# The opening of a fused attention and mixer kernel: batch 0's steps in another order, and no stuffing matmuls

## The chip, the cores and the metric

The kernel runs on one core of one Trainium2 chip. The metric is device time in microseconds (us) of one launch. Before the change it is 648.35 us, the median of three runs (647.37 to 651.1). The engines are called PE (matrix engine), ACT (scalar engine), DVE (vector engine), POOL (GpSimd) and SP (the engine that only issues DMA here).

## The reference, cut to what matters

Attention in chunks of 32 tokens is followed by a mixer. There are 4 batches, 8 heads, 768 tokens, a head size of 64 and 8 memory tokens.

```python
for c in range(nc):                      # chunks of 32; 16 tokens of left, 8 of right context
    k_full = concat([mem_k, k[:, :, l_start:r_end]]); v_full = concat([mem_v, v_ctx])
    scores = scale * (q_c @ k_full.T)
    a = exp(scores - max(scores)); a = a / (sum(a) + 1e-9)
    out[:, :, c] = a @ v_full
x = out.transpose(0, 2, 1, 3).reshape(B, S, 512)
h = x.T @ U @ V                          # U: 768 x 32, V: 32 x 768, double precision inputs
u = x + h.T
result = u + relu(u @ w_ch1) @ w_ch2     # 512 -> 2048 -> 512, double precision inputs
```

U, V and the two weight matrices arrive as 64-bit numbers. The kernel decodes them to 32 bits on the chip with integer and multiply operations.

## The kernel before, in words

The kernel has a front, in which the attention of batch 0 is computed, and a long rest, in which the mixer of one batch runs beside the attention of the next. The front is the function `attention` with `b == 0`. It handles batch 0 in three parts T = 0, 1, 2 of 256 tokens, each with two halves h of four heads.

For each part the front goes through these steps. `regroup` lays out the raw k or q. `turn` transposes it on PE into a PSUM bank. `k_part` copies it to the context tile `kall` with ACT (lines 664 to 672), and `q_part` copies q (line 688). In `k_part` the copy at line 668 writes "edges": the first tokens of part T that are the right context of the last block of part T - 1. `s_turn` computes scores of one part on PE (line 708). `s_weights` takes the maximum and subtracts it on DVE (lines 730 and 731) and takes the exponential on ACT (line 734). `s_sums` sums rows on DVE (lines 739 to 744). `t_part` transposes one half of the probabilities on PE (line 762) and copies them with ACT (line 765). `av_part` multiplies with v on PE (line 782) and scales into the tiles x on DVE (line 794); each part gives two tiles x of 128 tokens.

With x the front goes on to the mixer. `collect(t)` (line 806) adds u times one x tile to the accumulator acc2. `turn_x` (line 1151) turns the first three x tiles, 12 matmuls, into the banks ps_h, ps_h, acc0 and acc1, and `turn_x1` (line 1175) the other three for one column block. `spread_v` (lines 292 to 298) copies the decoded v of the mixer onto three partition groups. `join_uT` (lines 1160 to 1165) joins the turned x with g, the collected product (lines 1100 and 1101); `join_uT1` does so for the second half (lines 1192 to 1197). The first hidden products follow (line 1501).

The class `Words` decodes 64-bit numbers: `begin` on ACT (line 240), `shift`, `power` and `mantissa` on DVE (lines 247, 255, 260), `join` (line 267). U, V and the weights pass through it. The weights go through the generator `stream`; `advance(n)` makes n steps of it. Step 1 is `begin` of the first weights, steps 2 to 5 decode them and write the upper part (line 397), the next step writes the lower part (line 401).

The order of the work is written out in the front. PE and SP keep the order of the program everywhere. ACT and POOL keep it in the front and for the first two units of the mixer (`HEAD`), DVE for the first 27 (`PACED`); after that a planner with its own estimates orders them. PSUM banks in the front come from a fixed cycle: `cyc = ["a", "h", "a", "o0", "a", "h", "o1"]`, where a is a pool of three banks ps_a, h a pool of two banks ps_h, and o0 and o1 are acc0 and acc1. Once `wide[0]` is set to None, all banks come from ps_a.

Stuffing matmuls multiply a tile of zeros. `keep_clock(n)` asks for n of them, and the next `att_ps()` puts them in front of its own work (line 143). There are 12 at the very start (`START`), two before the scores of part 0, two before those of part 1, two before the last product with v (`GAP`), and eight before `turn_x1` (`CHAIN[0]`).

The loads are issued by SP in the order of `LOADS`: q and k of the three parts, u and v of the mixer, the attention's v of the parts 0, 1 and 2 (v0, v1, v2, lines 610 and 617), then weights (lines 344 and 356). `take(n)` issues the next n of this list.

## Time and profile before

| | us |
|---|---|
| median of three runs | 648.35 |
| the three runs | 651.1, 647.37, 648.35 |
| the profiled execution's own time | 648.01 |
| its span, first to last instruction | 645.9 |
| PE busy | 619.7 |
| DVE busy | 379.5 |
| ACT busy | 252.5 |
| POOL busy | 137.5 |

All times of the trace count from the start of the span. A wait carries the name of what ended it. "issue" stands for time in which the engine waited for nothing that the profile shows. Ends of matmuls are modelled, so neighbouring matmuls overlap by a few tenths of a microsecond in a timeline.

### The profile page before, as it was taken

Reading aid. Unit: us, or ns where it says so; the run is one execution under the profiler, and the core shown is the slowest. Engines: PE = TensorE matmul, PEld = TensorE weight load, DVE = VectorE, ACT = ScalarE, POOL = GpSimd, SP = SyncE. Lnnn points to the kernel's source line nnn. Section 1 sums busy time; section 2 is a strip of 40 time slices with the busy share of each in tenths; the row PEclk is TensorE's granted clock in tenths of the full one; section 3 lists DMA queues with packets and bytes.
Section 4 is the critical chain, followed back from the end, with each engine's and each line's share of the span. In section 5 each row is a group of like instructions: output and inputs, shape, how many; then the busy total and the mean of one; then the engine's idle time right before and its main releaser. Section 6 shows DMA issues by size and latency. Waiting matters only on the chain.

```text
span 645.9 us, 15115 instructions
## 1 busy us (share of the span) xinstructions
PE 619.7 (96%) x6006; PEld 536.3 (83%) x6006; DVE 379.5 (59%) x727; ACT 252.5 (39%) x635; POOL 137.5 (21%) x292
## 2 busy tenths in 40 slices
PE   7788999999899999899999999999999999999997
PEld 5557999988787888779889798998877899999886
DVE  6948788798783737954755834653456732222322
ACT  5525445448332535522255613321247621221221
POOL 5100000043154454312734100202325200000000
PEclk9899999999999999999999999999999999999999
DMA  8895576667888699576589759767422065565201
GB/s 240 160 335 200 170 253 231 224 184 179 184 187 214 167 298 280 179 188 162 169 244 207 160 158 284 228 175 200 117 68 96 0 185 175 146 175 155 96 0 49
DMA packets 168705, 115.02 MB, mean 178 GB/s; under 512 B 100956, under 2 KB 139484, under 8 KB 168636
## 3 DMA queue, kind: packets, MB, share of 16 engines
q1 hardware_dynamic: 168012, 113.92, 62.3%
q8 instruction: 47, 0.77, 0.5%
q10 hardware_dynamic: 624, 0.15, 0.1%
q14 instruction: 22, 0.18, 0.1%
HBM read 90.83 MB, written 28.97 MB: 185 GB/s over the span
## 4 chain that ended last, share of the span: by engine, by line
PE 74%; DVE 9%; DMA 6%; ACT 5%; issue 2%; POOL 2%; SPq 1%; ACTq 0%; POOLq 0%; DVEq 0%
PE ps_h L1321 23%; PE acc L1552 18%; PE acc L1562 9%; PE ps_h L1501 9%; PE ps_a L782 2%; DMA blocks<-spread 2%; PE ps_a L1552 2%; ACT uc L171 1%; PE acc L1546 1%; PE ps_a L708 1%; DMA w1l<-w1s 1%; PE ps_a L1562 1%; POOL pt L171 1%; DVE x L1517 1%; PE acc L806 1%
## 5 line engine op out<-in xcount | busy, mean ns | idle before, releaser
L1552 PE MATMUL acc<-w,hh 128*128 128x512 f32 x612 | 157.9, 393 | 1.3 <-ACT hh L1335 1.3
L1552 PEld LDWEIGHTS acc<-w,hh 128*128 128x128 f32 x612 | 113.3, 188 | 22.8 <-ACT hh L1335 2.8
L1562 PE MATMUL acc<-w,hl 128*128 128x512 f32 x306 | 86.9, 392 | 0.0
L1562 PEld LDWEIGHTS acc<-w,hl 128*128 128x128 f32 x306 | 56.9, 188 | 11.9
L1321 PE MATMUL ps_h<-t12h,w1l 128*128 128x384 f32 x192 | 55.5, 343 | 0.7 <-ACT c L1347 0.6
L1321 PE MATMUL ps_h<-bh,w1l 128*128 128x384 f32 x192 | 53.0, 340 | 0.0
L171 POOL COPY pt<-y 32x128 f32<-32x128 f32 x96 | 30.1, 314 | 98.5 <-DVE y L168 94.3
L1321 PE MATMUL ps_h<-t34h,w1l 128*128 128x384 f32 x152 | 46.1, 344 | 0.2 <-ACT hst L1347 0.2
L171 POOL COPY uc<-y 32x128 f32<-32x128 f32 x96 | 32.6, 340 | 56.8 <-DVE y L168 53.1
L1501 PE MATMUL ps_h<-uh,w1h 128*128 128x384 f32 x124 | 42.5, 347 | 2.2 <-ACT w1h L397 1.2
L1501 PE MATMUL ps_h<-ul,w1h 128*128 128x384 f32 x124 | 41.4, 338 | 0.4 <-DVE ul L1197 0.4
L1336 DVE SCALAR_TENSOR_TENSOR hl<-ps_h,hh 128x384 fp32r<-128x384 f32 x29 | 16.1, 554 | 43.0 <-ACT hh L1335 42.8
L1343 DVE TENSOR_TENSOR c<-ps_h,c 128x384 f32<-128x384 f32 x19 | 10.5, 554 | 49.7 <-PE ps_h L1321 49.7
L1321 PEld LDWEIGHTS ps_h<-t12h,w1l 128*128 128x128 f32 x192 | 35.3, 188 | 3.7 <-ACT c L1347 1.0
L1336 DVE SCALAR_TENSOR_TENSOR hl<-hst,hh 128x384 fp32r<-128x384 f32 x36 | 20.6, 574 | 30.0 <-PE acc L1562 21.3
L1321 PE MATMUL ps_h<-b,w1l 128*128 128x384 f32 x174 | 35.5, 339 | 0.7 <-DVE hst L1343 0.7
L1321 PEld LDWEIGHTS ps_h<-bh,w1l 128*128 128x128 f32 x192 | 35.1, 188 | 0.8
L1335 ACT ACTIVATE hh<-ps_h 128x384 fp32r<-128x384 f32 x29 | 14.2, 491 | 53.0 <-PE ps_h L1321 52.8
L1343 DVE TENSOR_TENSOR hst<-ps_h,hst 128x384 f32<-128x384 f32 x36 | 19.9, 553 | 23.8 <-ACT hst L1347 16.8
L1335 ACT ACTIVATE hh<-hst 128x384 fp32r<-128x384 f32 x36 | 18.8, 524 | 36.4 <-PE acc L1552 30.0
L1347 ACT COPY c<-ps_h 128x384 f32<-128x384 f32 x19 | 9.1, 479 | 59.5 <-PE ps_h L1321 59.5
L1321 PE MATMUL ps_h<-t12l,w1l 128*128 128x384 f32 x96 | 32.4, 337 | 0.0
(253 smaller groups left out, 1278.9 us busy)
## 6 DMA issues: line engine op xcount, KB each, us to landing
w1l<-w1s SPq DMA_DIRECT2D x155, 256.0 KB
rw<-in_moe_w_ch_dram SPq DMA_DIRECT2D x14, 512.0 KB
out_dram<-x SPq DMA_DIRECT2D x24, 256.0 KB
blocks<-spread SPq DMA_DIRECT2D x24, 256.0 KB
vb<-in_v_dram SPq DMA_DIRECT2D x56, 98.0 KB
raw<-in_moe_w_ch_dram SPq DMA_DIRECT2D x20, 256.0 KB
rw<-in_moe_w_ch_dram SPq DMA_DIRECT2D x16, 256.0 KB
w1s<-sums SPq DMA_DIRECT2D x16, 256.0 KB
```

Of the source, the lines that this page charges most:

```text
L171: (nc.scalar.copy if both and (5 * to + at) % 8 < 3 else nc.gpsimd.tensor_copy)(out=dst[CK * to:CK * to + CK, :, CK * at:CK * at + CK], in ...
L708: nc.tensor.matmul(out=psv[s][(slice(CK * i, CK * i + CK), t) + ((p // 2, p % 2) if b >= DIRECT else (p % 2, p // 2))], lhsT=qt[p // 2][ro ...
L782: nc.tensor.matmul(out=psv[g][CK * i:CK * i + CK, t, j], lhsT=pt[s][rows, 2 * t + k_, CK * i:CK * i + CK], rhs=vt[rows, NI * t + i, D * j: ...
L806: nc.tensor.matmul(out=gp[0][0:96], lhsT=u3[:, t].rearrange("p g r -> p (g r)"), rhs=xs[(b, t)], start=(t == 0), stop=(t + 1 == NT),)
L1321: nc.tensor.matmul(out=ps[:, :TOK], lhsT=w_, rhs=u, start=(start and m == 0), stop=(m == 5), skip_group_check=True,)
L1335: nc.scalar.activation(out=hh, in_=c, func=AF.Relu)
L1336: nc.vector.scalar_tensor_tensor(out=hl, in0=c, scalar=0.0, in1=hh.bitcast(F32), op0=ALU.max, op1=ALU.subtract,)
L1343: nc.vector.tensor_tensor(out=out, in0=ps[:, :TOK], in1=in1, op=ALU.add)
L1347: nc.scalar.copy(out=out, in_=ps[:, :TOK])
L1501: nc.tensor.matmul(out=ph[:, :TOK], lhsT=w[:, c, :], rhs=u[c], start=(m == 0), stop=(m + 1 == len(parts)),)
L1552: nc.tensor.matmul(out=acc[tt], lhsT=h[:, sl], rhs=w, start=(begins and m == 0), stop=False,)
L1562: nc.tensor.matmul(out=acc[tt], lhsT=hl[:, sl], rhs=w2h[f], start=False, stop=ends is not None)
```

## The change

The instructions that compute are the same, apart from 14 stuffing matmuls that are left out: 2, 2, 2 and 8. The 12 at the start stay.

- `k_part` is split. `k_edges` turns a half of k on PE and, for T > 0, copies the edges. `k_main` makes the other copies. For parts 1 and 2 the edges of both halves are now copied before the rest of either half.
- The row sums of part 0 and the beginning of u's decoding move behind the softmax of part 1. The rest of u's decoding moves behind the softmax of part 2, around the product with v of part 0.
- The product with v of part 1 comes directly after the turning of part 1's probabilities. Four `collect` follow it, then the row sums of part 2 and v's decoding, and only then the turning of part 2's probabilities. In the kernel before, v's decoding came ahead of that product's scaling on DVE, and the turning of part 2 ahead of the first collects.
- `turn_x` comes before `spread_v`, and `wide[0] = None` between them, so `spread_v` takes its three banks from ps_a.
- `advance(1)` and `advance(4)` become one `advance(5)` behind `spread_v`, ahead of the last product with v.

```diff
-GAP = [2, 2, 2]
-CHAIN = [8, 4]
...
+            k_main(T, h, k_edges(T, h))
+
+        def k_edges(T, h):
             psv = turn(kn.pop((T, h)))
+            m, w = NM // 2, CK // 2
+            last = kall[:, NB * ((T + 1) % 2) + NB - 1].rearrange("c p (n r) -> c p r n", r=2)
+            p = slice(2 * h, 2 * h + 2)
+            if T > 0:
+                nc.scalar.copy(out=last[:, p, :, m + w:], in_=psv[:, :, :, 0, 0:NW // 2 - m - w])
+            return psv
+
+        def k_main(T, h, psv):
             copy = nc.scalar.copy
...
             for h in two:
                 q_part(0, h)
+            made = [k_edges(1, h) for h in two]
             for h in two:
-                k_part(1, h)
+                k_main(1, h, made[h])
...
-            keep_clock(GAP[0])
             sc = s_turn(0)
             for h in two:
                 q_part(1, h)
+            made = [k_edges(2, h) for h in two]
             for h in two:
                 s_weights(0, *sc, [h])
-                k_part(2, h)
-            u_words.begin()
-            s_sums(0)
+                k_main(2, h, made[h])
             yield
-            keep_clock(GAP[1])
             sc = s_turn(1)
             for h in two:
                 q_part(2, h)
+            s_weights(1, *sc)
+            s_sums(0)
+            u_words.begin()
+            yield
+            sc = s_turn(2)
+            for s in two:
+                t_part(0, s)
+            s_weights(2, *sc)
             u_words.shift()
             u_words.low()
+            av_part(0)
             nc.vector.tensor_copy(
...
             nc.gpsimd.tensor_copy(out=u_sb, in_=u3[:, :, 0, :])
-            s_weights(1, *sc)
-            yield
-            sc = s_turn(2)
-            for s in two:
-                t_part(0, s)
-            s_weights(2, *sc)
-            v_words.begin()
             s_sums(1)
-            av_part(0)
             yield
             for s in two:
                 t_part(1, s)
+            v_words.begin()
+            av_part(1)
+            take(len(loading))
+            for t in range(4):
+                collect(t)
             s_sums(2)
             v_words.shift()
             v_words.low()
             val = v_words.join()
-            av_part(1)
-            take(len(loading))
             for s in two:
                 t_part(2, s)
-            for t in two:
-                collect(t)
+            early = turn_x(range(NCK))
+            wide[0] = None
             spread_v(val)
             yield
-            advance(1)
-            for t in two:
-                collect(2 + t)
-            early = turn_x(range(NCK))
-            wide[0] = None
-            keep_clock(GAP[2])
-            advance(4)
+            advance(5)
             av_part(2)
             yield
             advance(1)
             for t in range(4, NT):
                 collect(t)
-            keep_clock(CHAIN[0])
             turned.extend(turn_x1(c) for c in range(3))
```

## Rows read from the trace of the kernel before

**Rows 1.** The page's head and first part: busy time by engine.

```profile
span 645.9 us, 15115 instructions
PE 619.7 (96%) x6006; PEld 536.3 (83%) x6006; DVE 379.5 (59%) x727; ACT 252.5 (39%) x635; POOL 137.5 (21%) x292
```

**Rows 2.** Busy time by stretch: stretch, length, engines, granted clock, DMA share and GB/s.

```profile
0.00:60.00 60.00, 47.77 (x972) 34.57 (x973) 41.77 (x100) 26.98 (x77) 11.62 (x22) 0.97 0.82 240
...
sum 646.00, PE 619.70 PEld 536.31 DVE 379.55 ACT 252.53 POOL 137.47; mean PE 47.67 PEld 41.25 DVE 29.20 ACT 19.43 POOL 10.57
```

**Rows 3.** Chain of waits, 0 to 62 us: start, duration, what.

```profile
28.94 0.96 issue
...
41.06 0.43 PE ps_a L143 x2
41.49 1.48 PE ps_a L782 x91
42.98 0.75 DVE x L794 x2
...
45.73 1.73 PE ps_a L143 x8
...
49.46 0.19 PE ps_h L1160
```

**Rows 4.** Timeline of PE: start, duration, instruction; idle time before it in brackets.

```profile
18.29 0.24 PE L708 MATMUL ps_a<-kall,qt 64*32 64x64 f32 x1 [1.23 <-ACT kall L668]
...
31.33 0.66 PE L762 MATMUL ps_a<-ident,pt 128*128 128x128 f32 x4
33.57 0.60 PE L762 MATMUL ps_h<-ident,pt 128*128 128x128 f32 x4 [1.59 <-issue]
...
35.82 0.45 PE L292 MATMUL ps_a<-dec,rep 32*96 32x256 f32 x1
...
36.43 0.67 PE L806 MATMUL acc<-x,uarea 128*96 128x512 f32 x1
```

**Rows 5.** Timeline of ACT: copy of part 1's second half of turned probabilities.

```profile
28.49 0.58 ACT L765 COPY pt<-ps_a 128x512 f32<-128x512 f32 x1
```

**Rows 6.** Timeline of DVE.

```profile
18.65 0.26 DVE L247 TENSOR_SCALAR dec<-dec 128x192 int32<-128x192 int32 x1 [0.26 <-ACT dec L240]
...
20.23 0.46 DVE L894 COPY uarea<-dec 128x576 f32<-128x576 f32 x1
...
29.36 1.27 DVE L739 TENSOR_REDUCE rs<-pt 128x8 f32<-128x512 f32 x2
...
32.42 0.41 DVE L794 TENSOR_TENSOR x<-ps_h,rs 128x256 f32<-128x256 f32 x1
...
37.27 0.41 DVE L298 TENSOR_TENSOR v<-acc,v 32x256 fp32r<-32x256 f32 x1
...
39.84 0.69 DVE L267 TENSOR_TENSOR dec<-dec 128x512 f32<-128x512 f32 x1
...
47.02 0.42 DVE L1101 TENSOR_TENSOR g<-acc,g 32x256 fp32r<-32x256 f32 x1 [0.43 <-ACT g L1100]
```

**Rows 7.** Timelines of SP's DMA issues and of POOL.

```profile
6.57 1.94 SPq L552 DMA_DIRECT2D kraw<-in_k_dram  x2
...
19.81 5.11 SPq L610 DMA_DIRECT2D vb<-in_v_dram  x8
...
11.83 1.36 POOL L577 COPY kn<-kraw 128x512 f32<-128x512 f32 x2 [2.52 <-DMA kraw<-in_k_dram]
...
18.89 0.40 POOL L636 COPY kall<-memkT 128x256 f32<-128x256 f32 x1 [0.90 <-PE ps_h L708]
```

**Rows 8.** Busy time and granted clock by stretch, as in rows 2.

```profile
21.20:24.60 3.40, 1.66 (x54) 1.21 (x39) 3.18 (x7) 1.87 (x4) 0.40 (x1) 1.00 0.74 146
24.60:28.00 3.40, 3.40 (x134) 3.17 (x135) 3.25 (x8) 2.00 (x5) 0.00 (x0) 0.50 1.13 173
...
31.40:34.80 3.40, 1.81 (x10) 1.22 (x11) 2.36 (x7) 1.17 (x2) 0.00 (x0) 1.00 0.70 192
```

## The prediction

> **What bounds the kernel now.** I read four views. The page comes first [rows 1]: TensorE (PE) is busy for 619.7 of 645.9 us, so the kernel as a whole is bound by PE and little can be won elsewhere. Then the table by stretches [rows 2], for where PE is not busy: in the first 60 us it works 47.77 us, and in the 586 us behind them 619.70 - 47.77 = 571.9 us. So 12.2 us of idling lie in the front, which the change rewrites, and 14.1 us behind it. Behind 60 us PE runs almost without a gap, so what the front gains or loses in time is kept to the end. Third, the chain of waits through the front [rows 3]; the reader is to see which pieces of it are stuffing (L143), which are waits called "issue", and where it passes to the vector engine (DVE). I take as the front's end mark the first matmul of line 1160, at 49.46 us in that chain: there the turned x of batch 0 meets g, and from there the instructions and their order are the same in both kernels. The forecast is how far this mark moves. Last, each engine's timeline around these pieces [rows 4 to 7] and the granted clock [rows 8].

> I count against the profiled execution's own 648.0 us (a span of 645.9 us and 2.1 us around it). It lies 0.34 us under the median of the three runs, 648.35.

> **Edges of k first, u's decoding later.** Today PE stalls 1.23 us before the last scores of part 1, until ACT has copied the edges of k's third part (L668), which stand behind a softmax and ten other copies [rows 4]. The edges now come first, so this stall goes. The decoding of u takes DVE from 18.65 to 20.69 us, ahead of part 1's softmax [rows 6]; it moves behind the softmax of part 2. Nothing is added: four edge copies and five decode operations are moved. With both out of the way, and the row sums of part 0 behind the second softmax too, I put part 1's turned probabilities some 3 us earlier: today the last of their copies ends at 28.49 + 0.58 = 29.07 us [rows 5], so about 26 us.

> What is late next? The product with v of part 1 also needs that part's v. Its eight transfers are issued until 19.81 + 5.11 = 24.92 us [rows 7], and nothing in the change moves them. No row says when the last one lands. The nearest rows are two transfers of k, issued between 6.57 and 8.51 us, for which POOL waits until 11.83 us [rows 7]: 3.3 to 5.3 us from issue to use. So v is there between 28.2 and 30.2 us. I take 29.65, near the late end, because the first product, today held to 29.90 by an "issue" wait [rows 3], can have had little to spare. So of the 3 us only a little arrives. Today the product restarts at 29.90 and PE is free for the next step at 31.33 [rows 3, 4]: 1.43 us for about 7/8 of it. In the new kernel three of its four head groups of the first half run while the last transfer comes, and 5/8 are left, 0.9 us: free at 30.55. Gain 0.78 us; from 0 to 1.5 us with the bounds of the landing and the stalls of today.

> **Products first, then the third part's turning.** Today PE then turns part 2's first half, waits 1.59 us on "issue" before the second half [rows 4], and does two collects, the spreading of v, two collects and the turning of x, until the stuffing at 41.06 [rows 3]. The new order is four collects, both halves, turning of x, spreading. The bank of the second half was released long before 33.57, so I read the 1.59 us as PE's own instruction stream; the four collects, slow and few, now stand in its place, and I count it as gone (kept, it costs 1.59 again). The collects of parts 2 and 3 of x need the products' scaling on DVE, which today stands behind row sums and v's decoding, 29.36 to 32.42 us [rows 6]; it now goes first, and is done under the first two collects. One new wait: the turning of x takes the bank of the second half, whose copy on ACT (0.58 us, as in [rows 5]) ends about 0.2 us late. The spreading, 36.43 - 35.82 = 0.61 us [rows 4], is moved behind. So the turning of x ends at 41.06 - 0.78 - 1.59 + 0.18 - 0.61 = 38.26 us, 2.8 us earlier, and the spreading starts there instead of at 35.82, 2.44 us later.

> **What comes of these 2.8 us.** Two things are queued behind the spreading. First, banks: it now takes three of the ps_a banks, and the last product with v follows on the first two of them. They come free with DVE's second subtraction, which today ends 37.27 + 0.41 - 35.82 = 1.86 us after the spreading begins [rows 4, 6]. So that product starts at 38.26 + 1.95 = 40.2 and ends 1.48 us later [rows 3], at 41.7: PE idles 1.3 us. Second, DVE: the decoding of the first weights is written between the spreading and the scaling of this product. It ends today 39.84 + 0.69 = 40.53, 4.71 us after the spreading's start [rows 4, 6], hidden under the turning of x; in the new order nothing covers it, and DVE is free for the scaling at 38.26 + 4.71 = 42.97 us. Today it starts at 42.98 [rows 3]. The whole gain up to here is given back: PE waits 2.1 us more instead. (With the landing at its bounds this term is -0.7 to +0.8 us; if the 1.59 us stay, +1.6.)

> **Stuffing out.** The two pairs before the scores of parts 0 and 1 stand before waits, and so does the pair at 41.06 now; they are worth nothing on the path. The eight at 45.73 take 1.73 us [rows 3] in front of the turning of x's second half, which needs only x. Without them the mark would be reached at 49.46 - 1.73 = 47.73. The other input there, g, is ready at 47.02 + 0.42 = 47.44 us [rows 6], just in time. So -1.7 us.

> **The clock.** At full clock the sum is -1.7 us. But PE gets two holes: from about 25 us until v lands at 29.65 it has only a few small matmuls, and from 38.9 to 43.8 us only the 1.5 us of the last product. [...] Here the path behind both holes is PE's own (collects, turnings), so each costs 0 to 1.7 us; I take 1.2 for the first, which can begin before v is there, and 1.1 for the second. [...]

> Sum: -1.7 + 1.2 + 1.1 = +0.6 us, so 648.6 us: no change.

> **Rivals.** (1) The clock stays up, or falls only inside the waits: 648.0 - 1.7 = 646.3, up to 647.2 with one stretch half paid. For it: the 1.81 busy us of [rows 8] that it survived. Against it: both holes are emptier than that. [...] (3) The rest is laid out otherwise. ACT and POOL are free of the written order from the third unit on, DVE from the 28th, and the planner already puts an instruction of batch 1 (POOL, L636) into the front at 18.89 us [rows 7]. With other times in the front it may order the rest otherwise. A gain cannot exceed the 14.1 idle us behind 60 us, and a loss has no row; I take 2 us either way, 646.6 or 650.6, and allow more in the tails. (4) The second hole is not there, because banks and decoding don't hold the scaling: PE would start the last product at 38.9 and its collects 2.4 us earlier, and with one low stretch paid the time is 648.6 - 1.1 - 2.4 = 645.1, at full clock 643.9. Against it: DVE's order is as written there.

> **Numbers.** Forecast 0.52, its own range 647.3 to 649.7; rival 1 0.16; rival 2 0.14; rival 3 0.12, half each way; rival 4 0.06. The range 645.9 to 651.0 leaves out rival 4, half of rival 3 and the upper end of rival 2, in all 0.17. A measurement can tell about 0.5%, 3.2 us, from no change: faster (under 645.1) is most of rival 4 and a tail of rival 3, 0.08; slower (over 651.6) the upper tails of 2 and 3, 0.09; the same 0.83.

> **What would show it.** No wait on L668 before the scores of part 1. PE nearly idle from about 25 us until close to 29.7, waiting for a transfer of v. Four collects in a row from 30.5 us. The last product with v starting some 2 us after the spreading, and its scaling directly behind DVE's decoding, near 43 to 44 us. Granted clock of 0.50 at some time in 27 to 34 and again in 42 to 48. The mark of line 1160 between 49.0 and 50.6 us. I am wrong in size if the clock stays at 1.00 (mark near 47.7), wrong in mechanism if the scaling starts well before 43 us, and wrong about what counts if the mark moves by one amount and the span by another.

## The result: 0.75% slower, with the front a little earlier

The changed kernel takes 654.09 us (median of 22 runs, 649.61 to 659.11), the kernel before 649.06 (22 runs on the same chips, 646.59 to 651.65). The ratio is 1.0075 [1.0053, 1.0096], some 5 us more. Forecast were 648.6 us and a range up to 651.0. Runs over 1.5% above the fastest of their kernel are left out of every ratio: none here, but of the kernels below six of 12 in e6, whose profile is of such a run, two of 12 in e5 and in e14 and one in e4 and in e11, and with them these five stand at 1.009, 1.002, 1.002, 1.019 and 1.002.

The page of the changed kernel, from an execution of 653.21 us: PE is busy as long as before [rows 1], and the span is 5.5 us longer. The last line is one of two queues that bring instructions; that it is PE's is worked out below. Its columns are packets, MB and the share of 16 DMA engines.

```profile
span 651.4 us, 15085 instructions
...
PE 620.5 (95%) x5992; PEld 537.0 (82%) x5992; DVE 381.5 (59%) x727; ACT 252.7 (39%) x635; POOL 139.2 (21%) x292
...
q8 instruction: 47, 0.77, 0.5%
```

**The front's order came as forecast.** The timeline of PE, to be read against [rows 3, 4]:

```profile
25.14 0.24 PE L788 MATMUL ps_a<-vb,pt 64*32 64x64 f32 x1 [1.50 <-issue]
...
29.08 0.21 PE L788 MATMUL ps_h<-vb,pt 64*32 64x64 f32 x1 [0.95 <-issue]
...
30.48 3.67 PE L812 MATMUL acc<-x,uarea 128*96 128x512 f32 x8
33.99 0.60 PE L768 MATMUL ps_a<-ident,pt 128*128 128x128 f32 x4
34.42 0.60 PE L768 MATMUL ps_h<-ident,pt 128*128 128x128 f32 x4
...
37.95 0.68 PE L290 MATMUL ps_a<-dec,rep 32*96 32x256 f32 x6
39.58 1.75 PE L788 MATMUL ps_a<-vbe,pt 64*32 64x64 f32 x128 [0.94 <-issue]
43.51 3.64 PE L812 MATMUL acc<-x,uarea 128*96 128x512 f32 x4 [2.18 <-DVE x L800]
48.91 0.60 PE L1161 MATMUL ps_h<-v,g 96*128 96x384 f32 x2
```

Collects from 30.48, the third part's turning in one piece, the spreading at 37.95, the last product with v at 39.58, then 2.18 us of waiting for DVE. DVE's own timeline shows what it waits for: the decoding of the first weights ends where the scaling begins.

```profile
41.98 0.69 DVE L265 TENSOR_TENSOR dec<-dec 128x512 f32<-128x512 f32 x1
42.70 1.42 DVE L800 TENSOR_TENSOR x<-ps_a,rs 128x256 f32<-128x256 f32 x4
```

The mark, the first matmul of the join, comes at 48.91 us; before, by the same view, at 49.22 (shown below with the waits of the kernel before). So the front gained 0.31 us in this pair of executions. That is inside the spread: in e10 and e13 below, whose front is that of the kernel before, the mark comes at 50.65 and 49.94 us, in e9 and e15, with the changed front, at 49.46 and 50.36.

**The loss lies behind the front.** DVE executes the same 727 instructions in both kernels, so one can be subtracted from its twin. After minus before, in us, at the time of before: -0.30 at 50; +0.68 at 65; +1.13 at 192; +2.67 at 199; +3.89 at 207; +4.2 at 277; +4.72 at 417; +5.84 at 443; +5.43 at 469 and no more change. On the way it also swings, as to +0.19 at 132 and +1.70 at 189. Three things make the lasting steps.

First, ACT near 63 us. The kernel before does the third unit's ReLU (hh) and then a cast of weights and three begins of decoding (first fence); the changed one does them the other way round (second fence).

```profile
63.20 0.49 ACT L1509 ACTIVATE hh<-ps_h 128x384 fp32r<-128x384 f32 x1 [0.93 <-PE ps_h L1501]
63.72 0.62 ACT L397 CAST w<-vb 128x512 fp32r<-128x512 f32 x1
```

```profile
63.41 0.62 ACT L395 CAST w<-vb 128x512 fp32r<-128x512 f32 x1 [1.46 <-DVE vb L265]
...
65.16 0.48 ACT L1510 ACTIVATE hh<-ps_h 128x384 fp32r<-128x384 f32 x1
```

The step is +0.98 us, from -0.30 to +0.68. Nothing in the source orders these two; the planner does, from its own times. ACT's order differs at two more places: among the copies of batch 1's k at 152 to 162 us, where `k_part` now makes a half's edge copy first, and at 194 us, where a cast now comes ahead of a copy of turned probabilities. PE's matmuls, subtracted in the same way, are 0.5 us late at 72 us and 0.5 us late at 195 us, so these two cost nothing that shows.

Second and largest, "issue" waits of PE among the small products with v of the other batches. Kernel before (its mark first), then the changed kernel:

```profile
49.22 0.42 PE L1160 MATMUL ps_h<-v,g 96*128 96x384 f32 x1
...
196.49 1.38 PE L782 MATMUL ps_a<-vb,pT 64*32 64x64 f32 x108
198.25 0.41 PE L782 MATMUL ps_a<-vb,pT 64*32 64x64 f32 x20 [0.38 <-issue]
...
442.07 0.56 PE L782 MATMUL ps_a<-vb,pT 64*32 64x64 f32 x29
```

```profile
196.98 1.64 PE L788 MATMUL ps_a<-vb,pT 64*32 64x64 f32 x122
200.93 0.43 PE L788 MATMUL ps_a<-vb,pT 64*32 64x64 f32 x6 [2.31 <-issue]
...
446.75 0.44 PE L788 MATMUL ps_a<-vb,pT 64*32 64x64 f32 x17
448.08 0.33 PE L788 MATMUL ps_a<-vb,pT 64*32 64x64 f32 x12 [0.90 <-issue]
```

Near 198 us it is the same run of 128 products, but it breaks after 108 in one kernel and after 122 in the other, and waits 0.38 or 2.31 us there. At 448 us, where the last 29 of such a run break into 17 and 12, the kernel before runs them in one piece. Counting PE's records in the trace (matmuls, weight loads and the semaphore records of its sequencer), the "issue" waits of over 0.2 us stand at numbers 193 or 194 (mod 256): before at 1217, 1473, 4802 and 10434, after at 449, 705, 962, 1217, 4801 and 9665. Two are not of this kind: 0.3 us at 154 us in both kernels, and the 0.94 us at 39.58 after, where the forecast has PE waiting for banks. Queue q8 brought 47 packets of 0.77 / 47 = 0.016 MB, and PE's 12,179 records are 47.6 times 256. So I count a block of 256 of PE's records for each packet. At the stop of 2.31 us PE had passed the border ahead at 196.00 us, the next packet of q8 began at 198.56 and took 1.23 us, and PE went on at 200.93; I read such a stop as a wait for that packet. The change takes 14 stuffing matmuls out of the front, 28 instructions and one semaphore record: every border behind the front moves by 29 instructions. Six of the changed kernel's 47 borders show an "issue" wait of over 0.2 us; the longest, 2.31 us at 200.93, ends a block of 122 small and 4 larger matmuls.

Third, the clock. From 200.53 to 203.94 us, over the end of the wait of 2.31 us and behind it, the granted clock was 0.50, with PE busy for 3.01 of 3.41 us; a stretch in the front likewise, in place of that of [rows 8]. A third, from 272.20 to 275.60 us, leaves PE 0.5 us later.

```profile
43.52:46.93 3.41, 3.41 (x4) 1.28 (x5) 1.19 (x3) 0.00 (x0) 0.00 (x0) 0.50 1.05 395
...
200.53:203.94 3.41, 3.01 (x14) 2.75 (x14) 2.08 (x6) 0.33 (x1) 0.33 (x1) 0.50 0.51 76
...
272.20:275.60 3.40, 3.40 (x80) 3.14 (x62) 2.59 (x7) 0.00 (x0) 0.00 (x0) 0.50 0.16 58
```

### The profile page after: what moved, and what is told of

Read it like the earlier page. It is cut to its first block, busy times and chain, and to the rows that moved or that the text cites. A ratio compares the mean times of both kernels' runs of the same rounds, so it can differ in the third digit from the quotient of the medians.

```text
span 651.4 us, 15085 instructions
## 1 busy us (share of the span) xinstructions
PE 620.5 (95%) x5992; PEld 537.0 (82%) x5992; DVE 381.5 (59%) x727; ACT 252.7 (39%) x635; POOL 139.2 (21%) x292
## 4 chain that ended last, share of the span: by engine, by line
PE 56%; DVE 5%; DMA 3%; ACT 3%; POOL 2%; issue 2%; SPq 2%; ACTq 0%; DVEq 0%; POOLq 0%
PE ps_h L1322 23%; PE acc L1553 16%; PE acc L1563 8%; PE ps_a L788 2%; PE ps_h L1502 2%; DMA blocks<-spread 2%; ACT uc L169 1%; PE acc L1547 1%; DMA w1l<-w1s 1%; POOL pt L169 1%; PE ps_a L714 1%; PE ps_a L818 1%; POOL vb L493 1%; DVE x L1518 1%; DMA w1s<-vb 1%
## 5 line engine op out<-in xcount | busy, mean ns | idle before, releaser
L169 POOL COPY pt<-y 32x128 f32<-32x128 f32 x96 | 30.2, 314 | 99.2 <-DVE y L166 95.0
L1344 DVE TENSOR_TENSOR c<-ps_h,c 128x384 f32<-128x384 f32 x19 | 10.5, 554 | 48.8 <-PE ps_h L1322 48.8
L575 POOL COPY kn<-kraw 128x512 f32<-128x512 f32 x8 | 8.3, 1039 | 112.5 <-DVE vb L258 102.2
```

The costliest lines, as they stand in the source:

```text
L169: (nc.scalar.copy if both and (5 * to + at) % 8 < 3 else nc.gpsimd.tensor_copy)(out=dst[CK * to:CK * to + CK, :, CK * at:CK * at + CK], in ...
L575: (nc.gpsimd if b == 1 or front[0] and T == 2 else nc.vector).tensor_copy(out=groups[T, h].rearrange("n r h d -> n h r d"), in_=raws.pop(( ...
L1344: nc.vector.tensor_tensor(out=out, in0=ps[:, :TOK], in1=in1, op=ALU.add)
```

## The experiments

All ratios are to the kernel before, run beside. "Borders" are PE's block borders behind the front, counted in PE's records against the kernel before; "ReLU late" is ACT's order of the changed kernel. The wait is that at the border near 200 us in the profiled execution; the lag is the time from PE's crossing of the border ahead to the start of the packet it then waits for.

| kernel | borders | ReLU | ratio [95%] | wait us | lag us |
|---|---|---|---|---|---|
| before | 0 | old | 1 | 0.38 | 1.98 |
| after | -29 | late | 1.0075 [1.0053, 1.0096] | 2.31 | 2.56 |
| e1 | -1 | late | 1.0043 [1.0014, 1.0073] | 3.28 | 5.54 |
| e2 | -28 | late | 1.0042 [1.0014, 1.0070] | 3.16 | 3.21 |
| e3 | +67 | old | 1.0144 [1.0117, 1.0170] | 2.57 | 4.53 |
| e4 | +207 | old | 1.0169 [1.0142, 1.0196] | 2.31 | 2.42 |
| e5 | -1 | old | 0.9999 [0.9971, 1.0026] | 0.66 | 3.15 |
| e6 | -29 | late | 1.0043 [1.0012, 1.0074] | 3.70 | 3.82 |
| e7 | -1 | late | 1.0079 [1.0054, 1.0104] | 3.57 | 5.84 |
| e8 | +255 | late | 1.0105 [1.0074, 1.0137] | 0.93 | 2.73 |
| e9 | -29 | late | 1.0095 [1.0061, 1.0129] | 2.57 | 2.52 |
| e10 | 0 | old | 1.0013 [0.9997, 1.0029] | 0 | 1.95 |
| e11 | -1 | old | 1.0012 [0.9987, 1.0037] | 3.62 | 5.67 |
| e12 | -1 | old | 1.0037 [1.0019, 1.0055] | 2.80 | 4.94 |
| e13 | 0 | old | 0.9989 [0.9972, 1.0006] | 0.39 | 2.47 |
| e14 | -1 | old | 1.0009 [0.9977, 1.0040] | 3.58 | 6.10 |
| e15 | -29 | late | 1.0094 [1.0058, 1.0129] | 2.75 | 2.84 |
| e16 | -1 | old | 1.0019 [0.9994, 1.0043] | 0.93 | 3.26 |
| e17 | -1 | old | 0.9997 [0.9978, 1.0016] | 1.21 | 3.65 |
| e18 | -1 | old | 1.0026 [1.0001, 1.0052] | 3.07 | 5.25 |

**e1, e3, e4, e8: moving the borders.** The changed kernel with small fp32 matmuls ahead of the last product with v; they write the product's bank before it does, and nothing reads them. One counts as four of PE's instructions: e1's seven move the borders from -29 to -1. n = 7, 24, 59 and 71 in e1, e3, e4 and e8.

```diff
+        for n in range(tiny[0]):
+            nc.tensor.matmul(
+                out=ps[CK * (n % 4):CK * (n % 4) + CK, 0:64], lhsT=ident[0:64, 0:CK], rhs=ident[0:64, 0:64],
+                start=True, stop=True,
+            )
+        tiny[0] = 0
...
+            tiny[0] = 7
             av_part(2)
```

> The changed kernel with 7 tiny fp32 matmuls (32 by 64, 28 PE instructions, well under 1 us) in PE's own wait ahead of the last product with v of batch 0; every other engine's order is as in the changed kernel. Theory 1, PE's instruction stream: PE's code comes in blocks of 256 instructions, a block is fetched while the one before it runs, and a block run through in less than some 4.5 us makes PE wait. Leaving out 14 stuffing matmuls (28 instructions) moved the block borders of all later code into the dense small matmuls of batches 1 and 3. Putting 28 instructions back puts the borders back: the waits of 2.31 us at 200.9 and 0.90 us at 448.1 in the changed kernel's trace go, and the time falls by 3.5 to 5 us to 649 to 650.5, ratio to the kernel before 1.000 to 1.003. Theory 2, the planner's other order on ACT behind the front: nothing changes, 654, ratio 1.0075. Theory 3, the clock falls because the stuffing is gone: 0.2 us of tiny matmuls don't hold a clock, 653 to 654.

> The changed kernel with 24 tiny matmuls (96 PE instructions) in the same place. The planner here keeps the ReLU of the third unit in its old place, worth -0.9 us. Theory 1: with a fetch of 4.5 us and the block times of the trace of the kernel before, the borders now fall worse than in the changed kernel: summed shortfall behind the front 10.5 us against 8.2 there and 3.3 before, so 654.1 + 2.3 - 0.9 = 655.5, ratio 1.010. Theory 2: 653.2. Theory 3: 653 to 654, or less, since PE has a little more to do in its wait.

> The changed kernel with 59 tiny matmuls (236 PE instructions) in the same place; they may fill up to 3 us of a wait of some 3 us there, so up to 1 us of them may be on the path. The ReLU of the third unit is in its old place. Theory 1: near the worst place of the borders, summed shortfall 14.4 us against 8.2: 654.1 + 6.2 - 0.9 = 659.4, ratio 1.016. Theory 2: 653.2 to 654.2. Theory 3: as theory 2 or less.

> The changed kernel with 71 small fp32 matmuls of 64 columns (284 of PE's instructions, 28 and a whole block of 256) ahead of the last product with v. In the front they cost what the 236 of e4 cost or more: some 1 to 2 us of work that is partly hidden behind DVE's decode, and a wait for the instructions of up to 4 us. Theory (block borders every 256 instructions): behind the join the borders lie at the same instructions as in e1 and as before the change, so from 60 us to the end it loses no more than e1, 2 to 4 us less than e3 and e4; the whole 652 to 656, ratio 1.005 to 1.012, below e4 (1.0169). Rival (the more instructions, the worse, or any new alignment is bad): 660 or more, 1.017 to 1.020, with long waits behind the join as in e4.

Measured: 651.95, 658.07, 659.89 and 655.52 us. So the time does not grow with the number of instructions: the 284 of e8 cost less than 96 or 236. e8's profile shows why. It has one packet more, and the run of 128 products breaks where it does in the kernel before, with 20 left; what e8 loses it loses in the front, at 47.95 us, where its own 71 small matmuls were run through.

```profile
q8 instruction: 48, 0.79, 0.5%
```

```profile
47.95 1.08 PE L795 MATMUL ps_a<-vbe,pt 64*32 64x64 f32 x52 [3.84 <-issue]
...
205.63 0.41 PE L795 MATMUL ps_a<-vb,pT 64*32 64x64 f32 x20 [0.93 <-issue]
```

e3 breaks elsewhere and adds two waits that no kernel with the old borders has, at 158 and 412 us:

```profile
158.16 0.31 PE L721 MATMUL ps_a<-kall,qt 64*32 64x64 f32 x5 [1.94 <-issue]
...
195.09 0.34 PE L795 MATMUL ps_a<-vb,pT 64*32 64x64 f32 x13 [2.57 <-issue]
...
411.97 0.44 PE L1330 MATMUL ps_h<-t34h,w1l 128*128 128x384 f32 x1 [1.17 <-issue]
```

The runs show a period of 256 instructions by that. The 4.5 us of these expectations are an estimate of mine: in the profiles before and after PE went on from nine of the ten stops listed above 3.67 to 5.20 us after it had passed the border ahead, and from the tenth after 2.19 us. e1, with the borders of before, won back less than half of the loss (its interval overlaps that of the changed kernel). The wait at 448 us is gone from its profile, as expected; the one near 200 us, which was to go too, stands at 3.28 us.

**e2: the stuffing alone.** The kernel before without its 14 stuffing matmuls, nothing else edited.

```diff
-GAP = [2, 2, 2]
+GAP = [0, 0, 0]
-CHAIN = [8, 4]
+CHAIN = [0, 4]
```

> The kernel before with its 14 stuffing matmuls left out and nothing reordered. Its planner puts one ReLU (third unit) behind three decode steps on ACT, as in the changed kernel (worth 0.9 us in that trace). Theory 1: the front wins 1.7 us (8 stuffing matmuls on the path), the ReLU costs 0.9, the moved block borders cost 4 to 5: 651.5 to 654, ratio 1.004 to 1.008, with a wait of 1 us or more near 198 to 201 us. Theory 2, the planner's ReLU alone: 649 - 1.7 + 0.9 = 648.2, ratio 0.999, or the reordering of the front is at fault and this is 647.3. Theory 3, the clock: about 1 to 3 us slower than before, with low clock in the first 60 us and not behind it.

651.89 us. DVE's work behind the join comes 2.96 us earlier than in the kernel before, and at the end it is 6.2 us behind: the borders have moved by 28, the planner has set the ReLU late here too, and the wait at 199 us is 3.16 us. So this part of the change by itself slows the kernel down, although it speeds the front up.

```profile
199.33 0.43 PE L782 MATMUL ps_a<-vb,pT 64*32 64x64 f32 x7 [3.16 <-issue]
```

**e5: borders and ReLU both as before.** e1 with matmuls of 128 columns; with these the planner sets the ReLU in its old place.

> The changed kernel with 7 small fp32 matmuls of 128 columns (28 of PE's instructions) ahead of the last product with v. They put every later instruction of PE back to within one of its old number, as e1 did with 64 columns, and with them the planner sets the third unit's ReLU back ahead of the cast and the three begins, as before the change, which it did not in e1. Theory (the borders of PE's instruction blocks, and the ReLU, 0.9 us): what was left of the loss in e1 was in good part the ReLU, so ratio to the kernel before 1.000 to 1.003, some 648.5 to 650.5 us, and PE's wait of 0.56 us at 70 us behind the cast is gone. Rival (the clock: without the 14 stuffing matmuls PE is idle longer in the front and pays later): as e1 or as the changed kernel, 1.004 to 1.0075. Rival (any move of the front against the transfers costs): 1.004 to 1.010.

649.26 us, 0.9999: the loss is gone. e14 and e17, which differ from e5 by one load of q on SP's queue, say the same (1.0009 and 0.9997). So with borders and ReLU as before, all the rest of the change, the front's new order included, is worth nothing within 0.4%. Page and PE's timeline of e5, from its fastest execution (643.91 us):

```profile
span 642.1 us, 15116 instructions
```

```profile
196.54 0.41 PE L795 MATMUL ps_a<-vb,pT 64*32 64x64 f32 x20 [0.66 <-issue]
```

**e6, e7, e11: the front made faster.** v's spreading goes ahead of the turning of x, so that DVE decodes under the turning (e6); e7 adds 14 stuffing matmuls ahead of part 1's products, e11 ahead of the last product. The edit of e11; that of e6 is the same without `keep_clock(14)`:

```diff
+            spread_v(val)
             early = turn_x(range(NCK))
             wide[0] = None
-            spread_v(val)
             yield
             advance(5)
+            keep_clock(14)
             av_part(2)
```

> The changed kernel with the spreading of v's halves (6 matmuls and their casts) ahead of the turning of x instead of behind it, so that DVE decodes the first weights only after v's last scaling and the last product's scaling does not wait for it. The number of PE's instructions stays that of the changed kernel. The first matmul of the join should come 2 to 4 us earlier than in the changed kernel (48.91 there). Theory (block borders): the borders behind the front lie as in the changed kernel, the waits near 200 and 448 us stay or grow by a part of what was won, since PE reaches the same borders earlier and the weights come no earlier: 651 to 654 us, ratio 1.003 to 1.008. Rival (the mark's shift is kept to the end): 654 less 2 to 4, 650 to 652 with the waits unchanged. If the gain were lost to the transfers of the weights, waits for DVE or for DMA would stand between 50 and 130 us.

> e6 with 14 stuffing matmuls (28 of PE's instructions) ahead of part 1's products with v, where PE waits for v to land. The join as early as in e6 or up to 1 us later; every later instruction of PE has its old number but one. Theory (block borders): the wait at 200 us is no longer than before the change and the one at 448 us is gone, so the front's gain is kept but for the ReLU's 0.9 us: 645 to 648 us, ratio 0.994 to 0.999. Rival (the clock alone): the stuffing keeps the clock up in the front, 1 us at most: 650 to 653. Rival (a gain in the front is always given back to the weights' transfers): 648 to 650, with waits for DVE or DMA ahead of 130 us.

> The changed kernel with the spreading of v ahead of the turning of x (as e6) and 14 stuffing matmuls ahead of the last product with v, where PE waits for banks and DVE. Every later instruction has its old number but one, and the ReLU stands in its old place. Theory (block borders, ReLU, and the clock: PE is busy through the stretch at 38 to 43 us that let it fall): join at 45 to 48 us, no low stretch there, waits at 200 as before the change or up to 3 us where the packet collides with the stores: 645 to 649 us, ratio 0.995 to 1.001, with a narrower spread of the runs than e5 had. Rival (the front's order itself costs, stuffing or not): 650 to 653. Rival (the 3 us of stuffing stand on the path in full): join at 48 to 50 us and 648 to 651.

654.46, 653.73 and 650.52 us. e6 brings the join's DVE work only 0.9 us earlier than the changed kernel, not 2 to 4: a border now falls into the last product, with a wait of 1.93 us at 42.83. e7 missed its forecast by 6 us: it has the old borders but the late ReLU, a granted clock of 0.93 over the first 50 us, and a wait of 3.57 us at 203. e11, with old borders and old ReLU, is back at the time of before, not below it, and it too had the long wait:

```profile
200.43 0.64 PE L788 MATMUL ps_a<-vb,pT 64*32 64x64 f32 x20 [3.62 <-issue]
```

**e9, e10, e12: is the packet behind the stores?** At 193.9 to 197.3 us in the kernel before SP issues four stores of weight sums, 1 MB, and the packet that PE then waits for begins at 195.03 us. e9 (from the changed kernel) and e12 (from e5) hold them back to the next group; e10 (from the kernel before) issues them twice. The edit of e10, then that of e9 and e12:

```diff
     def save_sums():
-        for p, i, pair in unkept:
+        for p, i, pair in unkept * (2 if unkept and unkept[0][0] == NF // 2 - 1 else 1):
```

```diff
     def save_sums():
+        if len(unkept) == 4 and unkept[0][0] == NF // 2 - 1 and not held_back[0]:
+            held_back[0] = 1
+            return
         for p, i, pair in unkept:
```

> The changed kernel with one group of four stores of weight sums (4 x 256 KB, issued at 194.98 us there) held back to the next group at some 211 us. PE's instructions and their numbers are those of the changed kernel; a few casts and copies behind 190 us change places. Theory (PE's instruction packet stands behind the transfers that fill the DMA engines at 195 to 200 us): the packet starts within 2 us of PE's crossing, the wait at 200.93 us falls from 2.31 to under 1 us and the low stretch of the clock behind it goes: 2 to 4 us, 650 to 652 us, ratio 1.002 to 1.005. Rival (the wait is given by how fast PE runs through the block alone): wait and time as in the changed kernel, 653 to 655. Rival (the loads of 128-byte pieces that then come earlier take the stores' place): packet and wait no better, 653 to 656.

> The kernel before with the same group of four stores (4 x 256 KB, issued at 193.93 us) issued twice, so 1 MB more to move at 194 to 200 us; every other instruction and order as in the kernel before. Theory (instruction packets queue behind transfers): the packet that PE needs at 198.25 us starts 2 to 3 us later, the wait there grows from 0.38 to 2 to 4 us, and the clock may fall behind it: ratio 1.003 to 1.008, 650 to 653 us. Rival (the wait is given by how fast PE runs through the block): the wait stays under 0.6 us and the time within 1 us of before, ratio 0.999 to 1.001; a loss would then show as waits for DMA of the weights or of q behind 200 us.

> e5 (borders as before the change, ReLU in its old place) with the group of four stores held back as in e9. Theory (instruction packets queue behind transfers): the wait at 197 us, 0.66 in e5's profile and by its alignment as long as 3.3 in e1's, stays under 0.5, and the time falls by 1 to 2 us against e5: 646.5 to 648.5 us, ratio 0.996 to 1.000, so at or below the kernel before. Rival (the wait there does not depend on the transfers, or others take their place): as e5, 649 us, 0.998 to 1.003. Rival (the changed places of casts behind 190 us cost): over 650.

The theory fell on all three. Without the stores the waits are 2.57 and 2.80 us, though the load that follows them on SP's queue moved up into their place there (in e9 to 195.25 us, ahead of PE's crossing); with them doubled there is none, and the 128 products run through in one piece:

```profile
197.93 1.66 PE L782 MATMUL ps_a<-vb,pT 64*32 64x64 f32 x128
```

**e13 to e18: is it the load of q behind the stores?** SP then issues a load of q in 3072 pieces of 128 bytes, 4.7 us after PE's crossing in the kernel before, 3.1 in e5, and more than 8 in e10. The edit of e13 to e16 (from before, e5, after and e11) was meant to place it behind the next load of weights; as the traces show, it moved a later load of q, from 209 to 214 us, and left this one. So these four only show how waits differ between executions of the like. e17 (from e5) and e18 (from e11) move the load itself. The edit of e13 to e16, then that of e17 and e18:

```diff
+            half_of(0)
             next(spreading)
-            half_of(0)
```

```diff
-SPREAD = {22: 1, 23: 1, 24: 1, 25: 1, 30: 1, 31: 1}
+SPREAD = {22: 1, 23: 1, 24: 1, 25: 1, 31: 2}
```

> The kernel before with one load of q (384 KB in 3072 pieces of 128 bytes, issued at 198.6 us there) placed behind the next load of weights on SP's queue, so issued some 2 us later. All else in the same order. Theory (the instruction packet that PE needs at 198 us is late where that load's pieces get ahead of it, and in the kernel before it nearly always comes first): nothing or little to win, ratio 0.998 to 1.000, wait there under 0.5 us. Rival (that load has nothing to do with it): 0.999 to 1.001 too, but then e14 and e16 gain nothing either. If the load is needed early by batch 3's front, 1.001 or more.

> e5 (borders and ReLU as before the change) with the same load of q behind the next load of weights. Theory: the packet starts 2 to 3 us after PE's crossing in every run, the wait near 197 us is 0 to 0.9 us, and the runs in which it was 3 us and the clock fell behind it are gone: 645.5 to 648.5 us, ratio 0.995 to 0.999, faster than the kernel before. Rival (the load does not matter; e5's spread comes from the clock in the front): as e5, 0.998 to 1.002, and the wait may be 3 us.

> The changed kernel with the same load of q behind the next load of weights. Its borders lie 29 instructions off, and PE runs through the block ahead of the wait in 2.4 us where the kernel before takes 4.6. Theory (both count: the packet in time by 2 to 3 us, but the block too short): a wait of 1.5 to 2.3 us stays at 200 us, so 652 to 654.5 us, ratio 1.005 to 1.008. Rival (that load alone makes the wait): the wait falls under 0.6 us and the ratio to 1.000 to 1.004.

> e11 (v's spreading ahead of the turning of x, 14 stuffing matmuls ahead of the last product, borders and ReLU as before the change) with the same load of q behind the next load of weights. Theory: the wait of 3.62 us at 200.43 us in e11's profile falls under 0.9 us and what the clock lost behind it comes back: 645.5 to 648.5 us, ratio 0.994 to 0.999. Rival (the load does not matter): the wait stays at 3 us or more and the ratio at 1.000 to 1.003.

> e5 (borders and ReLU as before the change) with the load of q that SP issues 3.1 us after PE's crossing at 191 us placed behind the next load of weights, some 7 us after the crossing. All else in the same order. Theory (that load's 3072 pieces of 128 bytes get ahead of the instruction packet in some runs): the packet starts 2 to 3.3 us after the crossing, the wait is under 1 us, and the runs in which it is 3 us and the clock falls behind it are gone: 645.5 to 648.5 us against 649 to 650 of e5 and its like, ratio 0.995 to 0.999. Rival (the load has nothing to do with it): packet and wait as before in some runs, 0.998 to 1.002.

> e11 (v's spreading ahead of the turning of x, 14 stuffing matmuls ahead of the last product, borders and ReLU as before the change) with the same load of q moved in the same way. Theory: a wait under 1 us near 200 us where e11's profile had 3.62, no low stretch of the clock behind it, 646 to 649 us, ratio 0.996 to 1.000. Rival (the load has nothing to do with it): a wait of 3 us in some runs, ratio 1.000 to 1.003 as e11 and e16.

e17 is no faster than the kernel before, and e18 has a wait of 3.07 us with the load out of the way:

```profile
200.91 0.64 PE L788 MATMUL ps_a<-vb,pT 64*32 64x64 f32 x20 [3.07 <-issue]
```

So this theory falls too, as far as one transfer at a time goes; no run took the stores and the load out together. What the table does show is a sum. PE goes on 1.1 to 1.7 us after the packet's end, and a packet takes 0.9 to 1.8 us. From one border to the next PE needs 4.6 to 4.9 us at the old borders (108 small products and 17 larger matmuls: 5.20 - 0.38 = 4.82 in the kernel before) and 2.6 at the new ones (122 small and 4 larger: 4.93 - 2.31). With a lag of 2 us that leaves no wait at the old borders and some 2 us at the new. With a lag of 5 to 6 us the old borders wait 3 us as well. Why the lag was 1.95 to 2.5 us in all three executions with the order of before and above 4.9 in six of ten with the changed front and the borders at -1 or +255 stays open.

The subtraction used above, done with PE's matmuls behind the mark for all 20 profiles, parts the pieces. From 49 to 72 us the eight kernels with the late ReLU lose 0.79 to 0.83 us each, and no other loses more than 0.02. From 195 to 206 us the five kernels with borders at -28 or -29 lose 2.5 to 5.0 us. Those with the old borders (0, -1 or +255) lose 4.0 to 5.9 us there in the six executions with a lag above 4.9 us, and at most 0.9 in the others. From 408 to 455 us the five lose 1.4 to 3.6 us and the old borders nothing. So the moved borders cost at both places in every profile; the old ones cost at one place, and there only when the packet is late, but then as much or more.

None of the versions beats the kernel before by a measurable amount; e13's 0.9989 [0.9972, 1.0006] includes 1.

## Why the prediction was wrong, step by step

**Edges first, u later: right.** No wait on the edges stands before part 1's scores. But the products with v did not wait for a transfer: the stops at 25.14 (1.50 us) and 29.08 (0.95 us) are "issue" waits at the borders 962 and 1217. PE went on at 29.08, not at 29.65. The landing of v, which I had bounded at 28.2 to 30.2, held nobody visibly; the stop that ends at 29.90 in the kernel before, from which I had placed it, is at border 1217 as well. That PE was free at 30.48 us (forecast 30.55) is luck: it went on 0.57 us earlier, and had 1.40 us of products left, not 0.9.

**Products first: right in sum.** Spreading at 37.95 (38.26). The 1.59 us before the second half of the turning are gone, and I had read them rightly as PE's instruction stream. I did not ask where that stream stops elsewhere: waits of 1.74, 0.85 and 1.50 us stand at 16.73, 20.40 and 25.14. The change did not make them: at the same three borders e13, with the front of before, waits 1.23, 0.86 and 0.75 us, e10 0.36, 0.28 and 0.20, and the kernel before less than 0.2.

**What comes of the 2.8 us: right.** The last product started at 39.58 (40.2), its collects at 43.51 (42.97 and on), behind the decoding of the first weights.

**Stuffing out, and the clock: right in sum, with one fall for two.** The granted clock fell once in the front, to 0.50 at 43.5 to 46.9 us; over the first hole and behind it, from 24.6 to 31.4 us, it was 1.00, with PE busy for 5.08 of 6.80 us. I had paid 1.2 us for the first hole and 1.1 for the second; no run shows these two terms. In their place this execution has one stretch of 3.41 us at 0.50, with PE busy all through it, worth at most half of that, 1.7 us by my estimate. In e9 and e15, which have the same front, it fell behind the second hole too, at 45.2 and 45.0 us, not behind the first, and once more near 18 us, where the forecast has no fall (e15 has a granted clock of 0.94 over the first 30 us and of 0.91 from 30 to 50 us). The mark came at 48.91 us by the timeline, on which the kernel before has 49.22. The 49.0 to 50.6 that I had given it count from 49.46, the chain's time of the same mark; on the timeline that is 48.8 to 50.4, and the mark is at its early end, 0.3 us earlier than before and not 0.6 us later. At full clock I had 1.7 us earlier; e5, with seven small matmuls more and the clock at 1.00 through its front, has the mark at 47.05, 2.2 us earlier.

**The step that failed** is the sentence "from there the instructions and their order are the same in both kernels", with "what the front gains or loses in time is kept to the end". PE's records behind the mark are the same 10,329, and in the same order. But their numbers in the stream are not, and with the numbers moved the places where PE stops for its next block. I listed the stuffing as worth "nothing on the path" or 1.7 us; its other effect, 28 instructions' worth of position, had no term. Of the 5.7 us between DVE's -0.30 at 50 us and +5.43 at the end, the late ReLU has 0.98, the wait at 200 us 1.54 (1.13 to 2.67; on PE 2.31 - 0.38 = 1.93), the low clock behind it 1.22, the wait at 448 us 1.12 and a step near 417 us, at another border (record 8897), 0.5; the rest is small steps. Read on PE itself, the ReLU has 0.80, the wait at 200 us with the low clock 3.40 and the borders near 417 and 448 us 1.62. The experiments agree in the main: the borders put back without the ReLU leave 1.004 to 1.008 (e1, e7); both put back leave 0.9997 to 1.0009 in e5, e14 and e17, and 1.0012 to 1.0037 in e11, e12, e16 and e18, which also reorder the front further or hold back the stores. The ratios alone do not divide the loss between borders and ReLU.

**The rivals.** Rival 3, the planner laying out the rest otherwise, did come, at half its price (0.98 of 2 us). Its chance of 0.12 was too small for a program of which one engine's order depends on times in another's. Rivals 1 and 4 both spoke of the front, which moved by a third of a microsecond. I had written that I would be wrong about what counts if the mark moves by one amount and the span by another. That is what happened.

**What stays open.** The ratios of e1 and e5 differ by 0.44% (2.9 us), and the late ReLU is worth 0.8 to 1 us of that. The clock in the front (0.93 and 1.00 over the first 50 us of the two profiles) does not account for the rest: e17's profile has 0.93 there too, and its last matmul comes 0.5 us earlier than in the kernel before. In the two profiles the rest lies at the border near 200 us, where PE loses 5.6 us in e1 (lag 5.54) and 0.3 in e5 (3.15). How often the long lag comes in the runs that were not profiled, and what makes it long, no run shows. Nor did any run put the ReLU back and leave the borders at -29.

## What to carry to other kernels

An edit that adds or removes instructions on an engine moves all later ones in its stream: here the 28 instructions and one semaphore record that are gone move PE's borders by 29. Where that engine stops for its instructions ("issue" waits at a fixed distance, here 256), count the instructions of the edit, find which dense stretches the shifted borders fall into, and compare the time between two borders (2.6 us, or 4.6 to 4.9, near 200 us here) with the packet's lag (1.95 to 6.10 us). And where a planner orders an engine, compare that engine's order in both kernels before calling the rest unchanged.

## What was not expected of the hardware

```profile
200.43:206.00 5.57, 5.57 (x33) 4.79 (x33) 2.64 (x7) 0.49 (x1) 2.58 (x3) 0.50 0.28 65
```
